# GateLoop attention and maxout FFN on one core: the first two groups' decay sums without TensorE's identity products, and every step list and PSUM room in another order

## The chip, the cores and the metric

One core of one Trainium2 chip runs the whole program in one launch. The metric is the device time of that launch in microseconds (us). Inputs and output are float32.

## The reference, cut to what matters

```python
# attention: batch 4, heads 8, seq 768, head_dim 48
mag = np.sqrt(a_re * a_re + a_im * a_im)
scale = np.minimum(mag, 0.999) / (mag + 1e-06)
a_re_n, a_im_n = a_re * scale, a_im * scale
for t in range(S):                                  # S_re, S_im: 48 x 48 per head
    S_re, S_im = ar * S_re - ai * S_im + kv, ar * S_im + ai * S_re   # kv = outer(k[t], v[t])
    y[:, :, t] = q[t] @ S_re
# feed-forward on x = y as (3072 tokens, 384); w1, w2, w3 are 384 x 768, w_out 768 x 384
h = np.maximum(np.maximum(x @ w1, x @ w2), x @ w3)
return h @ w_out
```

A complex gate of modulus below 1 decays and turns a state along the sequence. The kernel takes logarithms and angles of the gates, sums them along the tokens with matrix products, and turns the recurrence into products of scaled queries and keys inside chunks of 64 tokens, with a state carried from chunk to chunk.

## The kernel before, in words

**Tiling.** Work comes in 12 groups g (two pairs of batches, six pieces of 128 tokens each). A group has two columns, "x" and "y", one per batch. A tile is 128 tokens by 384 (one column) or 768 (both).

**Steps.** Every step is a word "name:group", and SCHEDULE is the list of all 1858 words. `program` (line 926) hands them to `run` (882) in order. Class `Bound` (98) ties each instruction to the one before it on its engine, so the list is the order on every engine: PE (TensorE), DVE (VectorE), ACT (ScalarE), POOL (GpSimd) and SP (the loads and stores). An engine that waits holds up all that stands behind it in its list.

The words of a group, in the order of the data:

- Lr, Li, Lq, Lk, Lv load (SP). Gates, in `gates` (413), halves 0 and 1 apart in group 0: sqr, sqi, add, lnL, expe, expw, lne, relu, Lnop (the decay's logarithm), and xor, abs, half, pw or addw, lnw, expL, mulai, mulw, stt, atan, turn (its angle). The angle needs modulus plus |a_re|: w + e in group 0, w + L in the others.
- Angles, in `angles` (496): cs sums them along the tokens on PE; t, nf, af reduce them to a turn; sa, sb are the sines (ACT). Cd carries a row to the next group.
- Decays, in `turns` (537): sums and F on PE; En, Ek, Eq, f0 to f3 exponentials on ACT; mk, mq, uk, uq, kEn scale keys and queries on DVE; tpk, tpq transpose on PE; Kc, Qc copy the result out of PSUM. Q1, Q2, KB, QB, QG, in `factors` (607), are DVE products.
- Scores, in `scores` (638): A and B on PE; g0 to g3 and b0, b1 put them under masks. State: dk on PE, h0 to h3 on DVE. y on PE, x the copy of it.
- Feed-forward: U11, U12, U01, U02 are x @ w on PE (`up`), u11 to u02 the copies and maxima into hT or xhx; each covers half of the 768 columns or, in group 0, a third for one column ("U22y:0": the last third, third matrix, column y; `up_one`, 761; the tile is hT). The output product of groups 1 to 11 is done by seven products P1 to P7 (with S1 to S4 and J before them, Px, Py for 128 of the inputs, and r1, r6, r75, r57, ox, oy after them) in `seven` (817). In group 0 it is Ox:0 and Oy:0, nine products of 384 columns each (`project`, 862): three on x itself with a product of weights that T and M made, then six on hT, two for each third. D stores.
- W words bring the four weight matrices in and round them (Wa, a cast by `weight_step`, 347; We; Wg an addition). Z words clear buffers.

**What sets the order.** Beside SCHEDULE there are three tables. SLOTS gives each PSUM tile one of four rooms, in the order in which `banks` (124) is called; a room is taken again only after its last reader. OTHER names words that run on the other engine of two: ACT or DVE for copies, casts, relu, abs; POOL or DVE for clears; and for additions:

```python
159     def increase(out, in_):
161         if other():
162             dve.tensor_tensor(out=out, in0=out, in1=in_, op=OP.add)
163         else:
164             pool.dma_start(out=out, in_=in_, accum_op=OP.add)
```

QUARTERS names words whose product is issued as four of 32 output columns instead of one of 128 (`mmf`, 117; also cs and F). It is empty before.

**The words of the change.** With SUMS = 2 (line 84), groups 0 and 1 form the sum of the modulus in PSUM: `pw` multiplies w and e (or L) by the identity matrix, and lnw and mulw read the sum there. The other groups add in place by addw.

Of the kernel before, what the change touches and what calls it, by code (L numbers as in the profile page):

```python
# [969 lines left out]
```

## Time and profile before

| | |
|---|---|
| median of 3 runs | 555.67 us (555.03 to 556.41) |
| profiled execution | 555.11 us |
| its span, first to last instruction | 553.4 us |
| mean granted clock of PE | 0.988 |
| busy: PE, DVE, ACT, POOL | 524.8, 470.8, 369.7, 70.7 us |
| instructions: PE, DVE, ACT, POOL | 10086, 728, 653, 117 |
| chain of waits that ended last | PE 84%, ACT 5%, SP's queue 5% |

How to read it: the span is 1.7 us shorter than the execution's own time, which includes what lies around it. Busy time is a mean over stages, and the stages differ: in the first 90 us loads, gates and weights are brought up, later all groups run as a pipeline. A float32 product shows as two matmul instructions in the trace, so that a word of four products counts 8. Each instruction has the line 107, where `Bound` issues it, so groups are told apart by tile names: output, then inputs, as in "op<-wo,hT". The number after an idle time, as in "[2.53 <-ACT L L107]", is how long the engine sat idle before the instruction, and whose result ended that.

### The profile page before, as it was taken

The page shows a single profiled execution, that of the slowest core. Times are in us where ns is not written, and L with a number is a line of the kernel's source. Part 1 is how long each engine was busy: PE and PEld are TensorE (multiplying, and loading weights), DVE is VectorE, ACT ScalarE, POOL GpSimd, SP SyncE. Part 2 cuts the span into 40 slices and gives each one's busy share as a digit, 9 for nine tenths or more (in the row PEclk, how much of TensorE's full clock was granted, in tenths as well). Part 3 has the DMA queues.
Part 4 walks back from the last instruction along what each step waited for, and adds up shares of the span by engine and source line. Part 5 has one row for each costly group of instructions (what it writes and reads, how often), then busy time and mean ns, then how long its engine had stood idle before and what let it go on. Part 6 is the DMA issues. An engine that isn't in the chain of part 4 may idle for free.

```text
span 553.4 us, 22672 instructions
## 1 busy us (share of the span) xinstructions
PE 524.8 (95%) x10086; PEld 449.1 (81%) x10086; DVE 470.8 (85%) x728; ACT 369.7 (67%) x653; POOL 70.7 (13%) x117
## 2 busy tenths in 40 slices
...
DVE  4788889999999997999988888999999998887432
...
GB/s 227 272 236 195 168 125 80 51 128 63 108 40 122 69 67 53 61 44 89 80 111 58 35 102 129 64 91 52 67 123 18 32 107 70 3 31 2 31 1 28
...
## 3 DMA queue, kind: packets, MB, share of 16 engines
...
q14 instruction: 18, 0.15, 0.1%
...
## 4 chain that ended last, share of the span: by engine, by line
PE 84%; ACT 5%; SPq 5%; DVE 2%; DMA 2%; issue 1%; DVEq 0%; ACTq 0%
PE up L107 33%; PE op L107 24%; PE y L107 7%; PE A L107 5%; SPq L107 5%; PE tp L107 4%; PE dk L107 3%; PE cs L107 3%; PE sums L107 2%; PE F L107 2%; PE B L107 1%; DMA ar<-in_a_re_dram 1%; ACT L L107 1%; ACT L107 1%; DMA ai<-in_a_im_dram 1%
## 5 line engine op out<-in xcount | busy, mean ns | idle before, releaser
L107 PE MATMUL up<-xhx,w 128*128 128x256 f32 x792 | 177.0, 382 | 0.1
L107 PEld LDWEIGHTS up<-xhx,w 128*128 128x128 f32 x792 | 148.9, 190 | 21.2 <-PE B L107 0.3
L107 ACT ACT_TABLE_LOAD x49 | 62.9, 1283 | 1.6 <-PEq L954 0.8
L107 ACT COPY atm<-B 32x128 f32<-32x128 f32 x96 | 24.5, 255 | 36.6 <-DVE atm L107 19.1
L107 PE MATMUL op<-wo,xhx 128*128 128x192 f32 (+1 forms) x220 | 48.6, 364 | 0.0
L107 DVE TENSOR_TENSOR Q<-Q,f 112x1024 f32<-112x1024 f32 (+1 forms) x48 | 45.4, 953 | 2.1 <-ACT Q L107 1.2
L107 POOL DMA_DIRECT2D ar<-nf x40 | 34.6, 1304 | 60.5 <-DVE ar L107 49.2
L107 ACT ACTIVATE f<-F 48x232 f32<-48x232 f32 x96 | 34.4, 359 | 10.3 <-PE F L107 6.3
L107 PEld LDWEIGHTS op<-wo,xhx 128*128 128x128 f32 x220 | 36.5, 190 | 4.8 <-issue 0.8
L107 PE MATMUL y<-atm,vb 128*32 128x64 f32 x1152 | 39.3, 222 | 0.1
L107 PE MATMUL y<-QG,g 112*32 112x64 f32 x1408 | 38.1, 219 | 0.3 <-issue 0.3
L107 PEld LDWEIGHTS y<-atm,vb 128*32 128x32 f32 x1152 | 32.5, 110 | 5.4 <-issue 2.9
L107 PEld LDWEIGHTS y<-QG,g 112*32 112x32 f32 x1408 | 34.9, 110 | 0.5 <-issue 0.5
L107 DVE TENSOR_TENSOR ot<-ot,op 128x384 f32<-128x384 f32 (+1 forms) x56 | 25.6, 465 | 10.7 <-PE op L107 6.4
L107 PE MATMUL op<-wo,strassen 128*128 128x192 f32 x176 | 33.0, 331 | 0.0
L107 POOL DMA_DIRECT2D Ln<-e x9 | 8.3, 923 | 192.0 <-ACT e L107 73.7
L107 DVE COPY_PREDICATED atm<-masko,A 128x256 f32<-128x256 uint8 x72 | 31.3, 436 | 1.7
L107 PE MATMUL op<-w,strassen 128*128 128x192 f32 x176 | 32.2, 329 | 0.0
L107 PE MATMUL A<-Q,K 112*32 112x80 f32 x1536 | 31.6, 234 | 0.2 <-DVE Q L107 0.2
L107 PEld LDWEIGHTS A<-Q,K 112*32 112x32 f32 x1536 | 27.3, 110 | 3.0 <-issue 1.6
L107 ACT COPY Q<-tp 112x1024 f32<-112x1024 f32 x22 | 22.3, 1015 | 10.7 <-PE tp L107 10.6
L107 PEld LDWEIGHTS op<-wo,strassen 128*128 128x128 f32 x176 | 28.8, 190 | 0.8
...
## 6 DMA issues: line engine op xcount, KB each, us to landing
...
Ln<-e POOLq DMA_DIRECT2D x9, 384.0 KB, 4.3
w<-L POOLq DMA_DIRECT2D x7, 384.0 KB, 4.5
```

The costliest lines, as they stand in the source:

```text
L107: ins = f(*a, **kw)
```

## The change

SUMS becomes 0. So pw0:0, pw1:0 and pw:1 leave, addw0:0, addw1:0 and addw:1 come, and lnw and mulw read w in SBUF. All four tables are new: SCHEDULE has 1858 words again, in another order; SLOTS has 301 entries for 304; OTHER 74 words for 45; QUARTERS 45 for none.

```diff
 SCHEDULE = """
...
+relu0:0 lne0:0 Lnop0:0 WL0:0 Wa0:0 lnL1:0 expe1:0 abs0:0 half0:0 addw0:0 expw1:0 xor1:0 lne1:0 relu1:0 Lnop1:0 lnw0:0
...
 OTHER = set("""
-Zf:0 Zg:0 afx:0 relu:1 Qcy:0 addw:2 Lnop:2 Wg8:0 u21y:0 addw:3 relu:4 afx:3 abs:4 Lnop:4 u01:2 xx:3 afy:4 afx:5 addw:6 u01:4 afx:6 afy:6 abs:7 relu:8 Kcy:6 afy:7 afx:7 relu:9 abs:9 u11:7 u01:7 afx:9 Kcx:9 xy:8 u11:8 Kcy:9 afy:10 abs:11 Kcx:10 Qcy:10 Kcy:11 Kcx:11 xy:11 u01:11 u11:11
+Zf:0 Z0:0 Z1:0 Wa0:0 addw0:0 addw1:0 Wa3:0 ty:0 Wa9:0 relu:1 Qcx:0 Zg:0 addw:1 afy:0 Qcy:0 addw:2 Wa7:0 Wg7:0 u21y:0
+Wa8:0 Wg8:0 afy:1 Lnop:2 ty:2 relu:3 abs:3 addw:3 Kcy:2 afx:3 r1:1 xy:2 tx:4 afx:4 afy:4 Qcx:4 r1:3 afy:5 addw:6 xx:4
+u11:4 tx:6 abs:7 r1:4 afx:6 xy:5 u11:5 addw:8 xx:6 xy:6 u11:6 afy:8 afx:8 xy:7 addw:9 r1:6 afy:9 relu:10 r1:7 u11:8
+r1:8 tx:10 afx:10 abs:11 addw:11 u01:9 r1:9 xy:10 ty:11 u11:10 afx:11 Qcx:11 u11:11 u01:11 r1:11
 """.split())
 
 QUARTERS = set("""
+csx:2 csy:3 csx:4 csy:4 csx:5 Py:3 Px:3 csx:6 P5:4 csy:6 Py:4 Px:4 csy:7 Px:5 Py:6 P4:6 Px:6 P3:6 U01:7 P1:7 P5:7 Px:7
+Py:7 P6:7 P4:7 csy:10 P5:8 P1:8 P7:8 P4:8 csx:10 U01:9 U02:9 P6:9 P2:9 csx:11 csy:11 U11:10 U01:10 Px:10 Py:10 P4:10
+P5:10 P6:10 P7:10
 """.split())
...
-    SUMS, ADDS = 2, 1
+    SUMS, ADDS = 0, 1
...
         elif name == "addw":
             if g >= SUMS:
-                increase(w, L)
+                increase(w, L if g >= ADDS else e)
```

What the tables do is seen in the instructions, in program order on an engine. DVE near its start, group 0's gates, before (w<-pw,L is mulw; w_124 is a weight's We; ai and ar are the gates' parts):

```order
L107 ISA L<-L,e 128x384
L107 SCALAR_TENSOR_TENSOR ai<-ar,ai 128x384
L107 TENSOR_SCALAR ar<-ar 128x384
L107 SCALAR_TENSOR_TENSOR w_124<-w_125,xhx 128x3x256
L107 SCALAR_TENSOR_TENSOR Ln_111<-L,e 128x384
L107 SCALAR_TENSOR_TENSOR ai<-ar,ai 128x384
L107 SCALAR_TENSOR_TENSOR w_124<-w_126,xhx 128x3x256
L107 TENSOR_TENSOR w<-pw,L 128x384
```

and now, from the first Lnop to the second mulw:

```order
L210 SCALAR_TENSOR_TENSOR Ln_111<-L,e 128x384
L210 TENSOR_SCALAR xhx<-w_125 128x768
L210 TENSOR_SCALAR ar<-ar 128x384
L210 TENSOR_TENSOR w<-w,e 128x384
L210 SCALAR_TENSOR_TENSOR ai<-ar,ai 128x384
L210 SCALAR_TENSOR_TENSOR Ln_111<-L,e 128x384
L210 SCALAR_TENSOR_TENSOR w_124<-w_125,xhx 128x3x256
L210 TENSOR_TENSOR w<-w,e 128x384
L210 TENSOR_TENSOR w<-w,L 128x384
L210 TENSOR_TENSOR ai<-ai,L 128x384
```

The two sums w<-w,e are DVE additions, and a cast of the weights (xhx<-w_125, word Wa0) stands on DVE where ACT had it.

PE around Oy:0, before (the rows ahead of these are dkx:1; then tpqy:1, Ax:1, Oy:0, Fx:2, Bx:1, Ay:1):

```order
L107 MATMUL tp<-ident,uq_97 112x64 x16
L107 MATMUL A<-Q_121,K_119 32x80 x32
L107 MATMUL op<-wo,ot 128x384 x3
L107 MATMUL op<-wo,hT 128x384 x6
L107 MATMUL F<-cuts,Ln_111 48x29 x16
L107 MATMUL B<-QB,KB 32x32 x16
```

and now (Fy:1, U02y and U12y, U11y, tpkx:1, tpqx:1, U22y, Oy:0, tpqy:1, tpky:1, Ax:1, csx:2 in quarters, U22x, U21x):

```order
L210 MATMUL up<-ot,w_126 128x128 x12
L210 MATMUL up<-ot,w_125 128x128 x6
L210 MATMUL tp<-ident,uk_95 112x64 x16
L210 MATMUL tp<-ident,uq_96 112x64 x16
L210 MATMUL up<-ot,w_126 128x128 x6
L210 MATMUL op<-wo,ot 128x384 x3
L210 MATMUL op<-wo,hT 128x384 x6
L210 MATMUL tp<-ident,uq_97 112x64 x16
L210 MATMUL tp<-ident,uk_93 112x64 x16
L210 MATMUL A<-Q_121,K_119 32x80 x32
L210 MATMUL cs<-w,upto 32x192 x8
L210 MATMUL up<-ot,w_126 128x128 x6
```

Two transposes, Ax:1, a cs and two up words that stood ahead of Oy:0 now stand behind it, as do, out of these rows, dkx:1, sumsx:2, csy:2 and U12x.

PE's end, group 11, before (U01 and U11, U02, then P1, Px, P2, P5, P6, Py, P3, P7, P4):

```order
L107 MATMUL up<-xhx,w_125 128x256 x18
L107 MATMUL up<-xhx,w_126 128x256 x9
L107 MATMUL op<-wo,xhx 128x192 x4
L107 MATMUL op<-wo,xhx 128x384
L107 MATMUL op<-wo,xhx 128x192 x4
L107 MATMUL op<-wo,strassen 128x192 x4
L107 MATMUL op<-w_124,strassen 128x192 x4
L107 MATMUL op<-wo,xhx 128x384
L107 MATMUL op<-wo,strassen 128x192 x4
L107 MATMUL op<-w_124,strassen 128x192 x4
L107 MATMUL op<-w_124,xhx 128x192 x4
```

and now (U11, U12, Px, U01, U02, P7, P2, P5, P6, P1, Py, P3, P4):

```order
L210 MATMUL up<-xhx,w_126 128x256 x9
L210 MATMUL op<-wo,xhx 128x384
L210 MATMUL up<-xhx,w_125 128x256 x9
L210 MATMUL up<-xhx,w_126 128x256 x9
L210 MATMUL op<-w_124,strassen 128x192 x4
L210 MATMUL op<-wo,xhx 128x192 x4
L210 MATMUL op<-wo,strassen 128x192 x4
L210 MATMUL op<-w_124,strassen 128x192 x4
L210 MATMUL op<-wo,xhx 128x192 x4
L210 MATMUL op<-wo,xhx 128x384
L210 MATMUL op<-wo,strassen 128x192 x4
L210 MATMUL op<-w_124,xhx 128x192 x4
```

Px stands between the up words, and P7 is the first of the seven; P4 stays the last.

More of the change, by code (lines that the diff above doesn't have):

```diff
@@ new lines @@
+mkx:0 relu:1 sumsy:0 Eny:0 uqx:0 Wa6:0 We6:0 expe:1 expw:1 f2x:0 WL1:0 ukx:0 tpqx:0 tpkx:0 Qcx:0 f3x:0 abs:1 lne:1
+Zg:0 Lnop:1 Kcx:0 kEnx:0 Lvx:0 WL10:0 half:1 Eqy:0 addw:1 Lky:0 WL11:0 Lrx:2 Lry:2 afy:0 Eky:0 mqy:0 Q1x:0 Q2x:0 T0:0
+t0:0 lnw:1 expL:1 mulw:1 mulai:1 Cdx:0 dkx:0 Cdy:0 T1:0 Wa10:0 t1:0 M0:0 T2:0 QBx:0 We10:0 M1:0 stt:1 Wa11:0 Liy:2
+say:0 We11:0 mky:0 t2:0 h1x:0 h2x:0 Wa1:0 h3x:0 We1:0 QGx:0 sby:0 uqy:0 sqr:2 atan:1 WL2:0 Lix:2 Wa2:0 sqi:2 Fy:0
+f3y:0 add:2 lnL:2 f1y:0 Ax:0 M2:0 g0x:0 We2:0 Wg2:0 f2y:0 WL4:0 Wa4:0 f0y:0 m0:0 uky:0 tpky:0 tpqy:0 Kcy:0 g1x:0
@@ new lines @@
+turn:1 g2x:0 g3x:0 KBx:0 Bx:0 Qcy:0 WL5:0 Lvy:0 m1:0 b1x:0 relu:2 kEny:0 b0x:0 xor:2 Z3:0 Wg1:0 We4:0 Q1y:0 Wg4:0
+Q2y:0 csy:1 ty:1 csx:1 expw:2 Wa5:0 We5:0 Wg5:0 tx:1 yx:0 expe:2 xx:0 Lqy:1 WL7:0 Lky:1 sumsx:1 lne:2 QBy:0 nfx:1
+nfy:1 WL8:0 Lqx:1 Ay:0 g0y:0 abs:2 Eqx:1 afx:1 sumsy:1 half:2 dky:0 KBy:0 g1y:0 Enx:1 Eny:1 Ekx:1 Eqy:1 QGy:0 addw:2
+g2y:0 g3y:0 h1y:0 Eky:1 h2y:0 h3y:0 Cdy:1 Z4:0 Lkx:1 lnw:2 expL:2 mulai:2 Liy:3 Lix:3 mulw:2 stt:2 Lix:4 U02x:0 U01x:0
+u01x:0 By:0 b1y:0 U11x:0 b0y:0 yy:0 atan:2 Wa7:0 Cdx:1 We7:0 Wg7:0 sbx:1 Fx:1 xy:0 turn:2 u02x:0 mky:1 mqx:1 sax:1
@@ new lines @@
+u11x:0 sby:1 f2x:1 mkx:1 uqx:1 Lqx:2 Z2:0 Lvx:1 Lvy:1 Liy:4 U01y:0 f0x:1 u01y:0 f1x:1 U21y:0 u21y:0 Fy:1 ukx:1 mqy:1
+f1y:1 f0y:1 f3y:1 U02y:0 U12y:0 Wa8:0 We8:0 f2y:1 Wg8:0 f3x:1 u02y:0 h0x:1 h0y:1 afy:1 U11y:0 u11y:0 u12y:0 Lnop:2
+tpkx:1 tpqx:1 Qcx:1 QBx:1 Q1x:1 Q2x:1 U22y:0 QGx:1 u22y:0 Oy:0 Kcx:1 sqi:3 say:1 uqy:1 tpqy:1 uky:1 tpky:1 kEny:1 oy:0
+Qcy:1 Kcy:1 Q2y:1 Ax:1 g0x:1 Q1y:1 csx:2 tx:2 nfx:2 afx:2 U22x:0 U21x:0 g1x:1 g2x:1 g3x:1 u21x:0 sbx:2 KBx:1 u22x:0
+kEnx:1 Ay:1 Bx:1 b1x:1 b0x:1 dky:1 h1y:1 g0y:1 U12x:0 u12x:0 h2y:1 h3y:1 dkx:1 sumsx:2 Lry:3 Lkx:2 Lky:2 QBy:1 Lrx:3
@@ new lines @@
+sqi:4 Fy:2 atan:3 turn:3 add:4 b1x:2 f0y:2 f3y:2 lnL:4 h1x:2 h2x:2 mqy:2 b0x:2 f1y:2 f2y:2 h3x:2 Lrx:5 uqy:2 Lqy:3
+Lry:5 Dx:0 U12:1 u12:1 tpky:2 tpqy:2 csx:3 Qcy:2 Kcy:2 QBy:2 Q2y:2 tx:3 nfx:3 yx:2 xx:2 csy:3 expe:4 P1:1 S1:1 P5:1
+Q1y:2 KBy:2 kEny:2 lne:4 ty:3 nfy:3 Ay:2 By:2 S2:1 g0y:2 relu:4 afx:3 expw:4 Px:1 P6:1 P2:1 Py:1 afy:3 abs:4 g1y:2
+S4:1 g2y:2 g3y:2 sby:3 h0y:2 b1y:2 sax:3 b0y:2 xor:4 half:4 sbx:3 Lvy:2 dky:2 J4:0 sumsx:3 S3:1 P4:1 P7:1 P3:1 h1y:2
+h2y:2 QGy:2 h3y:2 Ekx:3 mkx:3 Eqx:3 r1:1 Lnop:4 Lvy:3 Dy:0 r6:1 r75:1 yy:2 ox:1 r57:1 Enx:3 oy:1 addw:4 lnw:4 say:3
@@ new lines @@
+expL:4 Cdx:3 Cdy:3 Fy:3 Fx:3 f2y:3 f1x:3 sumsy:3 f3y:3 Eqy:3 f3x:3 xy:2 U01:2 Eky:3 Eny:3 mulai:4 mqx:3 ukx:3 f2x:3
+f0y:3 sqr:5 mqy:3 uqy:3 mulw:4 Lky:3 stt:4 sqi:5 add:5 mky:3 uky:3 u01:2 uqx:3 U02:2 u02:2 f1y:3 h0y:3 f0x:3 tpky:3
+tpqx:3 tpqy:3 tpkx:3 Kcy:3 kEnx:3 S3:2 Qcx:3 Dx:1 Q1x:3 Qcy:3 Q1y:3 atan:4 Q2x:3 Q2y:3 QGx:3 QBx:3 turn:4 Lry:6 Kcx:3
+U11:2 lnL:5 u11:2 U12:2 u12:2 KBx:3 csx:4 csy:4 tx:4 expe:5 ty:4 nfy:4 expw:5 Ax:3 Bx:3 g0x:3 nfx:4 g1x:3 sby:4 relu:5
+afx:4 abs:5 sbx:4 sax:4 addw:5 P1:2 P7:2 S1:2 g2x:3 KBy:3 Lky:4 P5:2 Lqx:4 Dy:1 g3x:3 S2:2 Lqy:4 dkx:3 h0x:3 h1x:3
@@ new lines @@
+h0x:4 sqr:6 add:6 U01:3 u01:3 KBx:4 kEny:4 QGx:4 lnL:6 U02:3 csy:5 Lqy:5 Lky:5 Lvx:4 QBx:4 dkx:4 u02:3 S1:3 ty:5 nfy:5
+Fy:4 f3y:4 f1y:4 S2:3 f0y:4 f2y:4 h1x:4 h2x:4 Ax:4 csx:5 tx:5 Lqx:5 expe:6 Q2y:4 g0x:4 g1x:4 h3x:4 nfx:5 Q1y:4 afx:5
+relu:6 lne:6 Lnop:6 P7:3 P6:3 P5:3 S4:3 P1:3 Bx:4 g2x:4 g3x:4 KBy:4 QBy:4 xor:6 Ay:4 Py:3 Px:3 Dx:2 expw:6 abs:6 r1:3
+b0x:4 afy:5 b1x:4 addw:6 g0y:4 g1y:4 say:5 r6:3 r75:3 sax:5 lnw:6 yx:4 xx:4 Lix:7 g2y:4 half:6 Lvy:4 Lkx:5 r57:3 h0y:4
+g3y:4 QGy:4 P4:3 P3:3 P2:3 By:4 b1y:4 dky:4 sumsx:5 oy:3 h1y:4 b0y:4 expL:6 yy:4 ox:3 Ekx:5 Eqx:5 sumsy:5 mulai:6
@@ new lines @@
+mqx:5 xy:4 mulw:6 Eky:5 mky:5 sqi:7 mkx:5 stt:6 Lvy:5 Enx:5 h2y:4 h3y:4 atan:6 sby:5 U01:4 sbx:5 ukx:5 uqx:5 sqr:7
+Eqy:5 Lvy:6 turn:6 Lry:8 uky:5 xor:7 U02:4 Fx:5 add:7 u01:4 f1x:5 f3x:5 f0x:5 f2x:5 h0x:5 mqy:5 u02:4 uqy:5 Lrx:8
+Lky:6 Lvx:5 U11:4 u11:4 Dy:3 Eny:5 tpqx:5 Qcx:5 tpky:5 S3:4 tpkx:5 tpqy:5 Kcx:5 Q2x:5 Qcy:5 Kcy:5 Q1x:5 QBx:5 QGx:5
+kEnx:5 U12:4 u12:4 S1:4 KBx:5 Fy:5 dkx:5 f1y:5 f0y:5 S2:4 h1x:5 Ax:5 csx:6 tx:6 f2y:5 nfx:6 g0x:5 g1x:5 f3y:5 g2x:5
+Q2y:5 g3x:5 h0y:5 Liy:8 P5:4 Q1y:5 Lix:8 lnL:7 csy:6 ty:6 expw:7 Bx:5 P1:4 P6:4 relu:7 P7:4 expe:7 abs:7 KBy:5 b1x:5
@@ new lines @@
+Kcx:6 QBx:6 Kcy:6 Q2x:6 Qcy:6 Lrx:9 kEny:6 csx:7 Q1y:6 sqr:8 tx:7 nfx:7 sbx:7 KBx:6 U02:5 P1:5 u02:5 S1:5 S2:5 Ax:6
+add:8 g0x:6 csy:7 ty:7 Bx:6 lnL:8 expe:8 P6:5 P7:5 kEnx:6 P5:5 g1x:6 g2x:6 KBy:6 g3x:6 lne:8 expw:8 b0x:6 b1x:6 Dy:4
+nfy:7 Q2y:6 dkx:6 afy:7 QGx:6 S4:5 Ay:6 Px:5 Dx:4 r1:5 r6:5 g0y:6 r75:5 g1y:6 afx:7 g2y:6 relu:8 g3y:6 P3:5 Py:5 P2:5
+r57:5 QBy:6 By:6 h1x:6 h2x:6 yx:6 abs:8 addw:8 xx:6 say:7 sby:7 QGy:6 b1y:6 h3x:6 P4:5 oy:5 b0y:6 lnw:8 half:8 Cdy:7
+Cdx:7 dky:6 h1y:6 h2y:6 sumsy:7 Eky:7 Lix:9 Lqx:7 Lky:7 ox:5 Eqy:7 Eny:7 yy:6 xy:6 Fx:7 f1x:7 sumsx:7 Ekx:7 h3y:6
@@ new lines @@
+mky:7 uky:7 mkx:7 U01:6 expL:8 mulw:8 mulai:8 f0x:7 Enx:7 Eqx:7 f2x:7 mqx:7 mqy:7 stt:8 sax:7 uqx:7 ukx:7 Lvx:7 uqy:7
+atan:8 U11:6 u01:6 f3x:7 u11:6 h0x:7 Liy:9 Lix:10 Dy:5 tpkx:7 tpqx:7 tpky:7 Kcx:7 Lvy:8 tpqy:7 Qcx:7 Lkx:8 turn:8
+Lry:10 KBx:7 kEnx:7 Q2x:7 sqi:9 U12:6 Q1x:7 Lnop:8 sqr:9 Qcy:7 add:9 u12:6 Fy:7 dkx:7 Kcy:7 f3y:7 QBx:7 f1y:7 kEny:7
+h1x:7 h2x:7 h3x:7 f2y:7 f0y:7 Q2y:7 sumsx:8 Eqx:8 Enx:8 Ekx:8 U02:6 Q1y:7 u02:6 lnL:9 Ax:7 g0x:7 relu:9 g1x:7 g2x:7
+g3x:7 QGx:7 Bx:7 KBy:7 b0x:7 b1x:7 Py:6 P4:6 QBy:7 csx:8 csy:8 tx:8 nfx:8 Ay:7 Px:6 g0y:7 ty:8 nfy:8 afy:8 S1:6 yx:7
@@ new lines @@
+xx:7 g1y:7 g2y:7 S3:6 By:7 Lqy:8 P2:6 expe:9 h0y:7 Lqx:8 afx:8 lne:9 sax:8 g3y:7 S2:6 xor:9 Lvy:7 P7:6 P5:6 P6:6 Dx:5
+S4:6 QGy:7 dky:7 say:8 b0y:7 b1y:7 h1y:7 Liy:10 mqx:8 sbx:8 uqx:8 h2y:7 P3:6 h3y:7 sby:8 yy:7 Lky:8 xy:7 mkx:8 ukx:8
+expw:9 abs:9 half:9 Cdy:8 addw:9 lnw:9 expL:9 Lrx:10 Lqx:9 Lvy:9 P1:6 r1:6 r6:6 r75:6 r57:6 U11:7 u11:7 ox:6 Fx:8
+f0x:8 oy:6 mulw:9 f2x:8 f1x:8 tpqx:8 tpkx:8 mulai:9 Qcx:8 kEnx:8 f3x:8 QBx:8 h0x:8 sqi:10 Kcx:8 U01:7 Q2x:8 stt:9
+QGx:8 u01:7 Lvx:8 sumsy:8 dkx:8 Eny:8 Fy:8 Eqy:8 mqy:8 h1x:8 h2x:8 h3x:8 Cdx:8 Lnop:9 Eky:8 f2y:8 KBx:8 uqy:8 mky:8
@@ new lines @@
+Q1x:8 atan:9 sqr:10 add:10 f3y:8 f1y:8 lnL:10 uky:8 U12:7 u12:7 U02:7 f0y:8 turn:9 tpqy:8 tpky:8 Qcy:8 u02:7 S1:7
+Kcy:8 S3:7 Q2y:8 csy:9 csx:9 tx:9 Ax:8 Q1y:8 ty:9 nfy:9 sby:9 g0x:8 P7:7 g1x:8 nfx:9 g2x:8 Ay:8 Bx:8 QBy:8 S2:7 g3x:8
+b1x:8 afy:9 say:9 b0x:8 expe:10 KBy:8 g0y:8 g1y:8 P1:7 relu:10 P5:7 S4:7 afx:9 g2y:8 g3y:8 kEny:8 Px:7 Py:7 yx:8 P6:7
+expw:10 abs:10 addw:10 Dx:6 r1:7 Dy:6 By:8 b0y:8 xx:8 b1y:8 sbx:9 P2:7 P3:7 dky:8 sumsx:9 Ekx:9 Enx:9 Eqx:9 r6:7 r75:7
+r57:7 lne:10 QGy:8 Lky:9 Lry:11 h0y:8 xor:10 half:10 Cdx:9 h1y:8 P4:7 oy:7 h2y:8 yy:8 ox:7 xy:8 h3y:8 lnw:10 expL:10
```

51 lines of the change are left out of this document (46 added, 5 removed).

## The prediction

> **What bounds the kernel now.** I read the head of the page first, then its slices, then the busy time of each engine in chosen stretches (columns: stretch, its length, busy us of PE, PE's weight loads, DVE, ACT and POOL, granted clock, DMA share, GB/s).
>
> ```profile
> span 553.4 us, 22672 instructions
> PE 524.8 (95%) x10086; PEld 449.1 (81%) x10086; DVE 470.8 (85%) x728; ACT 369.7 (67%) x653; POOL 70.7 (13%) x117
> ...
> DVE  4788889999999997999988888999999998887432
> ```
> ```profile
> 0.00:10.00 10.00, 0.85 (x33) 0.83 (x33) 2.99 (x10) 7.11 (x15) 7.71 (x34) 1.00 0.84 224
> 10.00:20.00 10.00, 7.96 (x46) 4.03 (x46) 6.05 (x11) 9.60 (x22) 7.94 (x20) 0.83 0.95 251
> 20.00:30.00 10.00, 4.32 (x48) 3.27 (x47) 9.07 (x16) 9.97 (x14) 0.00 (x0) 0.97 0.92 244
> ...
> 92.00:152.00 60.00, 59.52 (x1252) 48.68 (x1244) 58.43 (x92) 46.55 (x85) 5.09 (x6) 1.00 0.46 87
> 152.00:238.00 86.00, 85.82 (x1787) 74.48 (x1785) 78.32 (x124) 66.60 (x112) 9.16 (x11) 1.00 0.34 67
> 238.00:538.00 300.00, 299.78 (x5810) 264.37 (x5807) 257.10 (x393) 172.18 (x312) 24.99 (x30) 1.00 0.31 62
> 538.00:553.40 15.40, 10.58 (x60) 9.42 (x58) 5.32 (x10) 0.32 (x1) 0.00 (x0) 1.00 0.08 26
> ```
> ```profile
> 0.00:93.19 93.19, 70.29 (x1198) 52.87 (x1199) 72.77 (x116) 85.27 (x147) 31.49 (x70) 0.93 0.81 189
> ```
>
> The reader is to see two stages. From 92 to 538 us PE is busy 445.1 of 446 us: nothing shortens that stage but less PE work or an earlier start. Up to 93.19 us PE has 22.9 us of idle time, ACT is full from 10 us on, and DVE idles 20.4 us, 10.96 of them in the first 20. So the end is the time at which PE's gapless stretch can begin, plus the PE work left there, plus the tail.
>
> As the mark between the stages I take the first group's output product, Oy:0: nine products, the last two of which need the rectified sum that DVE writes as u22y:0.
>
> ```profile
> 85.29 0.87 PE L107 MATMUL cs<-w,upto 128*64 128x192 f32 x8
> 86.09 3.10 PE L107 MATMUL up<-ot,w 128*128 128x128 f32 x24
> 89.12 1.14 PE L107 MATMUL dk<-vb,uk 64*64 64x48 f32 x64
> 90.19 0.66 PE L107 MATMUL tp<-ident,uq 64*112 64x64 f32 x16
> 90.79 1.31 PE L107 MATMUL A<-Q,K 112*32 112x80 f32 x64
> 92.03 2.20 PE L107 MATMUL op<-wo,ot 128*128 128x384 f32 x6
> ```
> ```profile
> 94.07 4.04 PE L107 MATMUL op<-wo,hT 128*128 128x384 f32 x12
> ```
> ```profile
> 92.79 0.40 DVE L107 TENSOR_TENSOR hT<-hT,up 128x256 f32<-128x256 f32 x1
> ```
>
> The six products on hT take 4.04 us, 0.66 each (start to start), so the last two begin at 94.07 + 4 x 0.66 = 96.7. DVE is done at 93.19: 3.5 us to spare.
>
> **The change, part by part.**
>
> **1. The identity products.** pw0:0, pw1:0 and pw:1 go.
>
> ```profile
> L107 PE MATMUL pw<-w,ident x8: 486/844/1007, 9.9 to 37.1; 128*128 128x384 f32 x8
> ```
> ```profile
> 15.48 1.48 PE L107 MATMUL pw<-w,ident 128*128 128x384 f32 x2 [2.04 <-ACT f L107]
> ```
>
> They lie between 9.9 and 38 us; 16 instructions of 0.486 to 1.007 us duration, in a stage where PE waits anyway. Their time is not on the path: I count 0 us (bounds: 0 to 10 us off PE, and the second only if PE bound that stage, which its 22.9 idle us deny). In their place DVE adds two 384-column tiles and one of 768 columns. They are not transfers: all three words stand in OTHER.
>
> **2. PE work behind the mark.** Nine words that PE did ahead of Oy:0 now come behind it: U12x, U21x, csx:2, csy:2, sumsx:2, tpky:1, tpqy:1, dkx:1, Ax:1. By the starts in the rows above, two up words are 3.03 us, a cs word 0.80, dk 1.07, tp 0.60, A 1.24; sums is 0.68 by this piece of the chain of waits:
>
> ```profile
> 198.82 0.68 PE sums L107 x16
> ```
>
> Sum 3.03 + 1.60 + 0.68 + 1.20 + 1.07 + 1.24 = **8.8 us more behind the mark**. Against it stand fewer changes of array shape: from Oy:0 on, consecutive words of unlike shape fall from 158 to 137, partly by order and partly because 45 words are issued in 32-column quarters.
>
> ```profile
> 155.78 1.50 PE op L107 x8
> ...
> 181.16 5.42 PE op L107 x32
> ```
>
> Four 192-column words take 5.42, one 1.50: three more cost 3.92, 1.31 each, so a change after such a run is 0.19 us. The mixed words behind the mark have no row that separates theirs so cleanly; I take a little less. 21 x 0.15 = **3.1 us less** (bounds 1, if a drained array hides behind loads, to 4.2 at 0.20). Left over: +5.7 us. [...]
>
> The quarters' own stream time I take as unchanged. Before has no quartered op; the nearest row is the y product, four 32-column tiles side by side:
>
> ```profile
> 152.40 1.72 PE y L107 x112
> ```
>
> 112 instructions with 112 loads of 32 columns in 1.72 us is 15 ns for each, though one load lasts 110 ns:
>
> ```profile
> L107 PEld LDWEIGHTS y<-atm,vb 128*32 128x32 f32 x1152 | 32.5, 110 | 5.4 <-issue 2.9
> ```
>
> So loads need not hold it up; a quartered op issues 32 in 1.31 us. Bounds: 0, to the rival below.
>
> **3. The tail.**
>
> ```profile
> 537.91 9.12 PE op L107 x52
> ...
> 547.05 0.57 DVE ot L107
> ...
> 547.64 0.56 DVE ot L107
> ...
> 548.25 1.58 PE op L107 x8
> ```
>
> PE waits 1.2 us for a PSUM room that two DVE sums free, before its last product. Now Px runs between the up words and P7 and P6 stand early, so rooms are freed further ahead; the last product keeps its place and the sum and the store behind it are the same. **-1.2 us** (bounds -1.2 to +0.6, one such DVE step waiting in a new place).
>
> Together: the end moves by (last two products of Oy:0 now) - 96.7 + 5.7 - 1.2. It breaks even if they start at 92.2.
>
> **4. When the mark is reached.** DVE's list ahead of u22y:0 grows. Prices, start to start, are about 0.08 below these mean durations:
>
> ```profile
> L107 DVE TENSOR_TENSOR QG<-Q,f 112x1024 f32<-112x1024 f32 (+1 forms) x24 | 27.1, 1130 | 0.0
> L107 DVE TENSOR_TENSOR w<-w,L 128x768 f32<-128x768 f32 x13 | 12.4, 953 | 0.3 <-ACT L L107 0.2
> ...
> L107 DVE COPY Q<-tp 112x1024 f32<-112x1024 f32 x2 | 2.4, 1222 | 0.5 <-PE tp L107 0.5
> ...
> L107 DVE TENSOR_SCALAR Ln<-L 128x768 f32<-128x768 f32 x4 | 2.2, 553 | 0.0
> ...
> L107 DVE MEMSET vb<- 128x768 f32 x2 | 1.4, 698 | 0.2
> ```
>
> New there: three adds 0.47 + 0.47 + 0.87; five weight casts (Wa) at 0.47 by the TENSOR_SCALAR row; two clears 0.62 each; Qcx 1.14; QGx:1 1.14; Wg7 0.87; h0y:1 0.47 and four small angle steps 0.27: 10.0 with rounding. Gone to behind the mark: three 768-column products, two nf, one mask, small ones, 5.2. Net **+4.8**, to 76.5 us from 71.8 (by starts). The casts are not shown on DVE before; a 768-column step there lies between 0.55 and 0.95 us, so +0 to +2 more.
>
> ACT's list ahead of the mark shrinks from 82.7 us of work by starts (its 85.27 busy us above, less overlaps) to 66.1: the five casts, two Q copies, two K copies and the angle and exponential steps of groups 1 and 2 stand on DVE or behind the mark now. A cast is
>
> ```profile
> 8.31 1.07 ACT L107 ACTIVATE xhx<-w 128x768 f16<-128x768 bf16 x1
> ```
>
> and DVE's idle time was mostly waiting on ACT:
>
> ```profile
> 5.50 0.56 DVE L107 CUSTOM_DVE_ANT_0 L<-L,e 128x384 f32<-128x384 f32 x1 [2.53 <-ACT L L107]
> 8.44 0.56 DVE L107 SCALAR_TENSOR_TENSOR Ln<-L,e 128x384 f32<-128x384 f32 x1 [2.38 <-ACT L L107]
> ...
> 17.70 0.56 DVE L107 TENSOR_TENSOR w<-pw,L 128x384 f32<-128x384 f32 x1 [2.34 <-ACT L L107]
> ```
>
> I take 9 us of idle for 20.4: the clears fill the start, and gate steps no longer queue behind casts on ACT, such as the one at 8.31. Bounds: 5 (no gate can reach DVE before 5.5) to 20.4 as now. DVE then does u22y:0 at 76.5 + 9 = 85.5, and PE starts the two products some 0.5 later, at 86.0. End: 86.0 - 96.7 + 5.7 - 1.2 = **-6.2 us**.
>
> **5. Given back.** From 92 to 152 DVE is busy 58.43 of 60 us, 1.6 to spare. A start 6 us earlier with a DVE list longer by some 10 us over the whole run makes PE wait there somewhere; what is queued behind such a wait is all of PE's list. I take **+2 us** (bounds 0 to 6).
>
> Sum: -4.2 against the profiled execution, whose own time is 555.11 us beside its span of 553.4; it would be 550.9. The median of before is 555.67, 0.56 above it, so 551.4.
>
> **The rivals.**
>
> (a) DVE keeps up everywhere, or idles only 5 us: without the +2, 549.5; with idle 5 another 4 less, 545.5. For it: ACT's 16.6 us fewer. Against: the slices of DVE stand at 9 from the seventh to the fifteenth, 83 to 207 us.
>
> (b) DVE becomes the bound. Place: DVE's list up to u22y:0. Price: its idle stays at 20.4, so the mark is 76.5 + 20.4 = 96.9, the products 97.4, and the end 97.4 - 92.2 = +5.2 us: 560.9. It decides from the mark later than 91.7, that is, idle over 15.2; each us more is a us of the kernel. For it: the loads of q, k and a run at a DMA share of 0.84 to 0.95 in the first 30 us, so gates can wait for data however free ACT is. Against: the rows above name ACT.
>
> (c) Idle around 12 and DVE late by 4 us in the busy stretch: all given back, -6.2 + 3 + 4 = +0.8, 556.5, and with a us either way 554 to 557.3.
>
> (d) The change doesn't do what it says: the sums as accumulating transfers, not adds. In before such a transfer lands 4.5 us after its issue, on the path of the first gates:
>
> ```profile
> w<-L POOLq DMA_DIRECT2D x7, 384.0 KB, 4.5
> ```
>
> Three of them are 13.5 us, less the DVE adds' 1.8; with a third of it on the path the mark comes 4 us later, and -4.2 + 4 leaves 555.5. The order shows adds, so this has little.
>
> (e) Quartered loads are not hidden: 32 loads of 0.110 us would make a 192-column word 3.5 us, +2.2 for each of 17, and the up words' 72 loads +3.8 for each of 5; with the rest some 58 us, 609. The y row, 15 ns a load in the same shape, speaks against it. [...]
>
> **How the numbers follow.** A measurement of this kernel can tell about 0.3%, 1.7 us: faster is below 554.0, slower above 557.3. Chances: forecast 0.52, (a) 0.13, (b) 0.17, (c) 0.15, (d) 0.02, (e) 0.01. Faster is forecast + (a), 0.65; within, (c) + (d), 0.17; slower, (b) + (e), 0.18. The range leaves out the far ends of (a) and (b): 546.5 to 558.5. Predicted: 551.4.
>
> **What would show it.** u22y:0 on DVE at 84 to 88 us with DVE idle under 12 before it (step 4); PE without gaps from there, DVE-caused waits of about 2 us between 90 and 200 (5); no gap ahead of PE's last product (3); one op word in quarters 1.3 us long and PE busy about 520 in all (2). The forecast is wrong if the mark comes later than 91 us, or if PE shows waits over 4 us behind it.

## The result, and the profile after

The changed kernel takes 551.87 us (median of 4 runs, 550.04 to 552.60) beside 555.53 for the kernel before on the same chip: a ratio of 0.9927, 95% interval 0.9899 to 0.9956. Measured once more, beside other executions of the kernel before, it took 551.40 for 554.40, a ratio of 0.9954 (0.9928 to 0.9980). So it is faster by 0.5 to 0.7%; 551.4 was forecast.

The head of the page and its slices, after:

```profile
span 550.9 us, 24305 instructions
PE 516.8 (94%) x10910; PEld 440.7 (80%) x10910; DVE 482.4 (88%) x757; ACT 367.9 (67%) x636; POOL 68.8 (12%) x112
...
DVE  6999798989999989989978999999979899989533
```

PE's busy time fell by 8.0 us, DVE's rose by 11.6, and the span fell by 2.5. DVE now stands at 6 tenths in the first slice and at 9 in the next three, where it stood at 4, 7, 8 and 8.

Busy time up to the mark (the end of u22y:0), the columns as before:

```profile
0.00:10.00 10.00, 0.61 (x8) 0.60 (x12) 5.60 (x15) 7.55 (x18) 7.69 (x32) 1.00 0.81 192
10.00:20.00 10.00, 3.10 (x52) 2.12 (x46) 9.89 (x19) 8.81 (x18) 8.77 (x20) 1.00 1.01 240
...
0.00:87.84 87.84, 59.84 (x974) 47.10 (x975) 77.39 (x124) 72.82 (x129) 30.82 (x67) 0.96 0.84 197
```

DVE is idle for 10.45 us ahead of the mark (20.4 before); in the first 20 us it idles 4.5 (10.96 before). The mark itself on DVE, and Oy:0 on PE:

```profile
87.42 0.42 DVE L210 TENSOR_TENSOR hT<-hT,up 128x256 f32<-128x256 f32 x1
```
```profile
84.23 2.10 PE L210 MATMUL op<-wo,ot 128*128 128x384 f32 x6
86.16 4.03 PE L210 MATMUL op<-wo,hT 128*128 128x384 f32 x12
```

Oy:0 starts 7.8 us earlier than before. Its last two products start at 86.16 + 4 x 0.66 = 88.8 (96.7 before). DVE was done with the mark at 87.84, 1.0 us ahead of them (3.5 before), so PE did not wait for it. The end of the chain of waits:

```profile
529.94 6.91 PE up L210 x32
536.85 9.77 PE op L210 x58
546.62 0.02 issue
546.64 0.55 DVE ot L210
547.20 0.27 DVEq L1068
547.46 0.26 DVE ot L210
```

There is no gap ahead of the last product any more, and PE ends at 546.62 (549.83 before): 3.2 us earlier.

What PE waited for, from 55 us on (columns: what waited, for whom; us in total, times, longest):

```profile
PE dk L210 <- issue: 3.6, 1, 3.6
PE A L210 <- ACT ot L210: 1.5, 1, 1.5
PE y L210 <- issue: 1.3, 2, 0.8
PE up L210 <- ACT ot L210: 1.0, 1, 1.0
PE sums L210 <- issue: 0.2, 1, 0.2
PE op L210 <- DVE nf L210: 0.2, 1, 0.2
```

Two things in this list matter. PE stood still for 5.1 us, most of it in the middle of words, with "issue" as the cause: it waited for nothing that the profile shows. Before, the same list has 0.8 us of that. And DVE, which was forecast to hold PE back for 2 us, did so for 0.2.

### The profile page after: what moved, and what is told of

Read it like the earlier page. It is cut to its first block, busy times and chain, and to the rows that moved or that the text cites. A ratio compares the mean times of both kernels' runs of the same rounds, so it can differ in the third digit from the quotient of the medians.

```text
span 550.9 us, 24305 instructions
## 1 busy us (share of the span) xinstructions
PE 516.8 (94%) x10910; PEld 440.7 (80%) x10910; DVE 482.4 (88%) x757; ACT 367.9 (67%) x636; POOL 68.8 (12%) x112
## 3 DMA queue, kind: packets, MB, share of 16 engines
q8 instruction: 86, 1.41, 1.0%
## 4 chain that ended last, share of the span: by engine, by line
PE 85%; ACT 4%; SPq 4%; DMA 3%; issue 2%; DVE 1%; DVEq 0%; ACTq 0%
PE up L210 34%; PE op L210 24%; PE y L210 7%; PE A L210 5%; PE dk L210 4%; SPq L210 4%; PE tp L210 4%; PE sums L210 3%; PE cs L210 2%; PE F L210 2%; PE B L210 1%; DMA wo<-in_moe_w_dram 1%; DMA strassen<-in_moe_w_out_dram 1%; DMA ai<-in_a_im_dram 1%; ACT L210 1%
## 5 line engine op out<-in xcount | busy, mean ns | idle before, releaser
L210 PE MATMUL up<-xhx,w 128*128 128x256 f32 (+1 forms) x1062 | 178.0, 382 | 0.0
L210 PEld LDWEIGHTS up<-xhx,w 128*128 128x128 f32 (+1 forms) x1062 | 144.8, 163 | 25.8 <-issue 1.0
L210 PE MATMUL op<-wo,xhx 128*128 128x192 f32 (+3 forms) x358 | 50.1, 380 | 0.2 <-DVE nf L210 0.2
L210 DVE TENSOR_TENSOR Q<-Q,f 112x512 f32<-112x512 f32 (+1 forms) x48 | 44.9, 953 | 0.8 <-ACT Q L210 0.7
L210 PEld LDWEIGHTS op<-wo,xhx 128*128 128x128 f32 (+1 forms) x358 | 35.0, 149 | 3.8 <-issue 0.9
L210 PE MATMUL op<-wo,strassen 128*32 128x192 f32 (+1 forms) x296 | 32.8, 328 | 0.0
L210 PE MATMUL op<-w,strassen 128*32 128x192 f32 (+1 forms) x296 | 32.1, 328 | 0.0
L210 PEld LDWEIGHTS dk<-vb,uk 64*48 64x48 f32 (+1 forms) x1408 | 24.6, 133 | 7.5 <-issue 6.9
L210 PE MATMUL dk<-vb,uk 64*64 64x48 f32 (+1 forms) x1408 | 27.1, 223 | 3.6 <-issue 3.6
L210 DVE TENSOR_TENSOR QG<-Q,f 112x1024 f32<-112x1024 f32 (+1 forms) x24 | 27.2, 1132 | 3.5 <-PE y L210 3.5
```

The costliest lines, as they stand in the source:

```text
L210: ins = f(*a, **kw)
```

## The experiments

Each kernel is the changed one with one edit, or the kernel before where that is said. The first four ask which part of the change carries the time, and whether the 3.6 us stall belongs to the kernel.

**again**: no edit.

> The changed kernel once more, nothing altered. In its first profile PE stood still for 3.6 us at 59.42 us in the middle of a dk word, with no semaphore to wait for, and ran at a granted clock of 0.56 to 0.67 for some 6 us behind it. If that stall belongs to the kernel, this profile shows it in the same place and the time is 551 to 553 us. If it comes and goes from one execution to the next, this profile may lack it; then u22y:0 comes 2 to 3 us earlier than 87.4 and the profiled execution takes 549 to 550 us.

551.40 us. The stall is there again, at 59.39 us and for 4.1 us, ahead of the same instruction of dky:0. It belongs to the kernel. PE's waits inside y at 110 and 114 us, 1.3 us in all, are not in this profile, so those come and go.

**no_quarters**

```diff
 QUARTERS = set("""
-csx:2 csy:3 csx:4 csy:4 csx:5 Py:3 Px:3 csx:6 P5:4 csy:6 Py:4 Px:4 csy:7 Px:5 Py:6 P4:6 Px:6 P3:6 U01:7 P1:7 P5:7 Px:7
...
 """.split())
```

> QUARTERS emptied, all else as in the changed kernel. My theory: a change of array shape costs PE 0.15 to 0.19 us and nothing hides it where PE has no gaps. Without quarters the changes from Oy:0 on go from 137 to 179, 42 more, so 6.3 to 8 us longer: 558 to 560 us. Rival one: the quarters do nothing (loads or drains hide): 552 us. Rival two: quartered loads cost time, then the kernel gets faster without them: below 550 us.

570.99 us, a ratio of 1.0284 (1.0244 to 1.0323) to before: 19.6 us slower than the changed kernel, over twice what any theory gave.

```profile
PE 523.8 (93%) x10070; PEld 446.2 (79%) x10070; DVE 483.9 (85%) x757; ACT 367.5 (65%) x636; POOL 68.7 (12%) x112
```
```profile
95.00:535.00 440.00, 430.49 (x8827) 370.31 (x8820) 389.11 (x608) 291.38 (x502) 37.99 (x45) 1.00 0.33 63
```
```profile
PE y L208 <- issue: 4.5, 7, 1.8
PE sums L208 <- issue: 2.7, 3, 1.0
PE dk L208 <- DMA vb<-in_v_dram: 1.6, 1, 1.6
PE dk L208 <- issue: 0.4, 1, 0.4
PE B L208 <- issue: 0.3, 1, 0.3
```

PE is busy 8.4 us more than in the profile of "again" (515.4). From Oy:0 on it is 9.3 us (469.28 for 459.99) for 42 more changes of shape, at most 0.22 us each. Part of it may belong to the idle gaps that follow here: the kernel "shifted_by_144" below has the same changes as "again", 13.2 us of such gaps, and is busy 4.3 us more (464.30). In proportion, 7.9 us of gaps would make 2.6 us of the 9.3 and leave 0.16 for a change, an estimate. Another 9.5 us is idle time between 95 and 535 us: 7.9 of it are "issue" waits in the middle of words, 1.6 a late load of v. The rival of unhidden loads is refuted by the changed kernel itself, in whose chain three quartered words of 192 columns stand together:

```profile
425.44 3.90 PE op L210 x96
```

They take 1.30 us each, as a whole word does (1.31): the 32 loads of 32 columns in each, 0.110 us long by the profile, are hidden. Without the quarters PE also has 1680 records fewer (20140 for 21820), which matters for the theory below, so this run alone does not say what the quarters are worth.

**sums_as_transfers**

```diff
 OTHER
-addw0:0 addw1:0 addw:1
```

> The three new sums leave the list of words that run on DVE, so they become accumulating transfers on POOL's queue. My theory: the gates of groups 0 and 1 wait for a landing of 4 to 6 us each where a DVE addition takes 0.5 or 0.9; with a third to a half on the path, u22y:0 comes 2 to 5 us later and the kernel takes 554 to 557 us. Rival: the path to u22y:0 does not go through these sums, and DVE is 1.8 us shorter: 550 to 552 us.

572.50 us, 1.0311 (1.0277 to 1.0345). What ACT and POOL did at the first sum:

```profile
11.12 0.51 ACT L211 ACTIVATE L<-L 128x384 f32<-128x384 f32 x1
23.90 0.52 ACT L211 ACTIVATE L<-w 128x384 f32<-128x384 f32 x1 [12.27 <-DMA w<-e]
```
```profile
16.27 1.03 POOL L211 DMA_DIRECT2D w<-e  x1
25.93 0.86 POOL L211 DMA_DIRECT2D w<-e  x1 [8.62 <-ACT e L211]
```

The sum was ready to be formed at 10.92 us, where DVE adds it in the changed kernel. As a transfer it is issued at 16.27, behind POOL's preparation of constants, and ACT, whose next step is the logarithm of it, stands still for 12.27 us with all that is queued behind. The second transfer waits for a step of that queue. My price, a landing of some 5 us with part of it on the path, had left out both queues. Oy:0 starts at 103.22, 18 us later than in "again" (85.05).

**two_weight_adds_on_dve**

```diff
 OTHER
+Wg4:0 Wg5:0
```

> Wg4 and Wg5, two additions of weight blocks which POOL issues as accumulating transfers at 54.73 and 57.33 us, run on DVE instead. If PE's stall at 59.42 us is an instruction fetch held up by the transfers (DMA share 1.19 at 54 to 60 us), it shrinks to under 1 us: 3 us saved, 1.7 us of DVE work added, so 550 to 551 us. If the transfers have nothing to do with it, the stall stays and the kernel takes 552 to 554 us.

551.25 us, 0.9937 (0.9910 to 0.9965): no different from the changed kernel. The stall in dky:0 shrank from 4.1 to 1.6 us, not to under 1. In the profile Oy:0 starts 3.6 us earlier than in "again" (81.44 for 85.05), but PE's last product ends only 0.8 us earlier: PE waits 2.1 us by "issue" between 95 and 535 us (0.3 in "again"). In the changed kernel the instruction queue's packet came 1.2 us after PE had stopped, with the DMA engines at this load (third and last but one columns: PE busy, DMA share):

```profile
54.00:60.00 6.00, 3.90 (x155) 3.15 (x144) 6.00 (x10) 6.00 (x12) 2.54 (x3) 1.00 1.19 192
60.00:63.01 3.01, 0.00 (x0) 0.00 (x0) 2.83 (x6) 0.72 (x2) 3.01 (x6) 0.78 1.11 294
63.01:69.00 5.99, 5.99 (x68) 5.90 (x69) 2.98 (x5) 2.44 (x4) 1.16 (x2) 0.54 1.08 243
```

Here, with two transfers fewer, the packet came at 59.99, 0.6 us earlier than in the changed kernel (60.62), and before PE stopped at 61.17. But PE itself stopped 1.8 us later, since it had waited for DVE, which now had the two additions to do:

```profile
PE sums L211 <- DVE nf L211: 1.5, 1, 1.5
```

So most of the shorter stall is PE's later arrival. That the load on the DMA engines makes the fetch late is not shown: in "shifted_by_32" below, at a share of 1.21 between 54 and 60 us, the packet came at 57.16 and this stall is absent. With the shorter stall, the low clock behind it is absent too: two up words take 2.94 us here at a granted clock of 1.00. In the changed kernel they take 4.87 right behind the stall, at 0.54, and 2.95 later:

```profile
64.46 4.87 PE L210 MATMUL up<-ot,w 128*128 128x128 f32 x24
```

**A theory for the stalls.** The instruction queue moved 86 packets and 1.41 MB after, 79 and 1.29 MB before:

```profile
q8 instruction: 86, 1.41, 1.0%
```

That is 16 KB a packet, and PE's 10910 products with as many loads come to 254 records for each (before: 20172 / 79 = 255). I counted PE's records ahead of each gap in the middle of a word. In "no_quarters" the counts, for "issue" gaps of 0.3 us and more from 60 us on, are 1202, 6033, 6540, 8323, 9595, 10103, 11628, 14425, 15693, 16712, 17474; modulo 256 they run 178, 145, 140, 131, 123, 119, 108, 89, 77, 72, 66, a slow drift along one lattice: from 1202 to 17474 is 64 steps of 254.25 records. In the changed kernel the gaps at 110 and 114 us lie at 2980 and 3236, 256 apart. With all of PE's records counted, those of semaphores too, they lie at 3009 and 3265, the stall in dky:0 at 1217, and the gap of before at 100.83 us at 2753: each is 193 modulo 256. So the theory is that PE fetches its instructions in pieces of 256 and stands still where a piece runs out before the next has come. By the starts of the packets, the next fetch begins 1.1 us (before) and 1.4 us (after) behind a piece's first record, in the median, and what it brings can be used some 2 us later, an estimate (the gaps listed here end 2.2 to 2.8 us after a packet's start, one 3.3); a piece filled with y, A, dk and F lasts less than that (224 records of y take 1.72 us), one with up and op words far longer (72 records of up words take 8.04 us at 413.30).

If so, the same order of work costs more or less time by where the borders fall. The next experiments move the borders by quartering early words, and test the parts of the change with the borders held as nearly as that allows.

**shifted_by_144, shifted_by_32, shifted_by_248**

```diff
 QUARTERS                        # one line each, in this order
+M0:0 M1:0
+csx:0 csy:0
+M0:0 M1:0 M2:0 csx:0 csy:0
```

> The changed kernel with M0:0 and M1:0 issued in quarters too: the same PE stream time, at 34 to 42 us, where PE waits for others, but 144 more PE instructions ahead of all the rest. My theory, formed on the runs before: PE fetches its instructions in pieces of 16 KB, 256 instructions, and stands still where a piece has run out in under some 3 us (dense words such as y, A, dk) before the next has come; what the order does to the time depends on where the piece borders fall. By the times of the pieces in the traces, a shift by 144 puts many more borders behind dense words: 5 to 9 us of PE stalls in the middle of words, 556 to 561 us. Rival: the stalls in the middle of words are DMA contention or chance; then the time stays at 550 to 552 us.

> The changed kernel with csx:0 and csy:0 in quarters: 32 more PE instructions ahead of the rest. Fetch theory: the borders move part of the way towards dense words; by the times of the pieces the stalls grow to between a third and a half of what 144 gave: 556 to 562 us. Rival: within 1.5 us of the changed kernel.

> The changed kernel with M0, M1, M2, csx:0 and csy:0 in quarters: 248 more PE instructions ahead of all the rest, eight short of a whole piece of 256. It quarters the two words of the run shifted by 144 and three more. Fetch theory: the borders fall 8 instructions from where the changed kernel has them, so the 19 us that the shift by 144 cost are gone: 550 to 553.5 us, at most 2.5 us of PE gaps in the middle of words from 70 us on. Rival: the quartered M words themselves, or the number of instructions, cost the time; then 568 us or more.

They took 570.32 (1.0289, 1.0260 to 1.0317), 556.78 (1.0044, 1.0018 to 1.0070) and 552.75 us (0.9948, 0.9916 to 0.9981). PE in the stretch from 95 to 535 us, for each in that order:

```profile
95.00:535.00 440.00, 426.06 (x9662) 366.76 (x9662) 389.71 (x610) 291.74 (x503) 37.99 (x45) 1.00 0.33 64
```
```profile
95.00:535.00 440.00, 433.91 (x9558) 371.93 (x9557) 389.77 (x609) 290.42 (x496) 38.06 (x45) 1.00 0.33 64
```
```profile
95.00:535.00 440.00, 438.89 (x9752) 377.92 (x9749) 395.73 (x620) 292.94 (x504) 38.06 (x45) 1.00 0.33 65
```

13.9, 6.1 and 1.1 us of idle time (0.55 in "again"). A shift by nearly a whole piece, with more quartered words than the shift by 144, has nearly the old time (552.75 for 551.40): the border's place decides, not the words. The counts ahead of the gaps lie on the old lattice (3236, 6289, 9851, 17481 in the shift by 144: 164, 145, 123, 73 modulo 256) while the work has moved along it. The shift by 144 costs 19 us in the medians, where I had said 5 to 9, and 16.5 in the profiled executions. There the idle time in this stretch is 13.4 us more, nearly all of it such gaps, and PE is counted busy 4.2 us more.

The shift by 32 shows something else as well. The border falls 32 records earlier in dky:0, the packet for it comes at 57.16 us (60.62 in the changed kernel), and the stall is absent: dky:0 starts at 59.43 (58.92 in the changed kernel), and yet Oy:0 starts 5.1 us earlier than in "again" (85.05):

```profile
79.99 2.10 PE L210 MATMUL op<-wo,ot 128*128 128x384 f32 x6
```

So the changed kernel itself loses some 5 us ahead of Oy:0 to this one stall, and the shift by 32 gains them there and loses more behind. Why the packet comes so late in the changed kernel stays open.

**before_with_adds, before_with_adds_same_borders**: the kernel before with the sums as DVE additions in the places of pw; in the second, the 32 PE instructions (16 matmuls and their 16 loads) that go with pw are made up. The three PSUM rooms of pw leave SLOTS in both.

```diff
-    SUMS, ADDS = 2, 1
+    SUMS, ADDS = 0, 1
...
-pw0:0 pw1:0 pw:1
+addw0:0 addw1:0 addw:1          # in SCHEDULE and in OTHER
...
 QUARTERS                        # the second kernel alone
+csx:0 csy:0
```

> The kernel before with one part of the change alone: SUMS 0, the three sums as DVE additions in the places of pw, its own order otherwise. First prediction's view: pw is not on the path and DVE has 1.8 us more, so 0 to +1 us against before. Rival one: PE bounds the kernel, so 5 us less PE work is 3 to 5 us less time. Rival two, the fetch theory: without pw, 32 PE instructions are gone ahead of all the rest, and the borders of the 16 KB pieces move by 32 towards dense words: some 4 us more PE stalls in the middle of words, so 3 to 5 us slower than before.

> As the run with the additions in the kernel before, but csx:0 and csy:0 in quarters, which adds 32 PE instructions near the start, so that the borders of the 16 KB pieces lie where they lay in before. Fetch theory and first prediction agree: 0 to +1 us against before, and no more than 1 us of PE gaps in the middle of words from 70 us on. Rival (PE work bounds): 3 to 5 us faster than before, here and in the run without quarters alike.

564.02 us (1.0166, 1.0140 to 1.0193) and 557.80 (1.0055, 1.0036 to 1.0075). PE from 95 to 535 us in the first and the second:

```profile
95.00:535.00 440.00, 432.04 (x8770) 375.44 (x8769) 388.92 (x599) 284.10 (x506) 39.23 (x47) 1.00 0.34 67
```
```profile
95.00:535.00 440.00, 439.49 (x8846) 382.41 (x8835) 391.59 (x604) 285.85 (x508) 39.23 (x47) 1.00 0.35 67
```

8.0 and 0.5 us idle. Of the 9.5 us that the additions cost in the old order, 6.2 are borders by these two times. The other 3.3 are the first stage: Oy:0 starts at 95.58 for 92.03. In the first kernel it starts at 93.51, so this division holds to some 2 us only, and quartering csx:0 and csy:0 may have a part in the 3.3. Both of my theories had 0 to +1 there, so both are off by 2 us; the rival by which 5 us less PE work is 3 to 5 us less time is refuted. The old order with this part of the change alone is slower than before.

**after_with_products, products_in_group_0_alone**: the other way round, pw back in the new order, for both groups or for group 0.

```diff
-    SUMS, ADDS = 0, 1
+    SUMS, ADDS = 2, 1           # group 0 alone: 1, 1
...
-addw0:0 addw1:0 addw:1
+pw0:0 pw1:0 pw:1                # group 0 alone: the first two
...
 SLOTS                           # rooms 6, 4, 4 for them
 QUARTERS
+M0:0 M1:0 M2:0
```

> The changed kernel with the identity products back in place of the three additions (PSUM rooms 6, 4, 4), and M0, M1, M2 in quarters, so that 248 more PE instructions stand ahead: nearly a whole piece of 256, the borders almost where they were. My view: PE has the room for 5 us more before 55 us, DVE has 1.8 us less, lnw waits for PE instead; the time is within 2 us of the changed kernel, 549.5 to 553.5. Rival: the gain of the change is the 5 us of PE work that it removes; then 555 us or more.

> The changed kernel with the identity products back in group 0 alone (SUMS 1, PSUM rooms 6 and 4), group 1's sum a DVE addition as in the changed kernel; M0, M1, M2 in quarters, so that 232 more PE instructions stand ahead, 24 short of a piece, where the times of the pieces give no more stalls than now. With all three products back the kernel took 561 us, and DVE stood still for 6.2 us at 35.4 waiting for group 1's logarithm behind pw:1. If that one product is the cost, this run takes 551 to 554 us. [...]

561.08 us (1.0110, 1.0077 to 1.0144) and 558.38 (1.0054, 1.0025 to 1.0084). The first shows a wait that I had not priced. The last of the three products on PE, and DVE behind it:

```profile
33.52 1.65 PE L229 MATMUL pw<-w,ident 128*128 128x384 f32 x2 [2.45 <-ACT Ek L229]
...
37.52 0.99 PE L229 MATMUL pw<-L,ident 128*128 128x384 f32 x2
```
```profile
41.63 0.96 DVE L229 TENSOR_TENSOR w<-pw,L 128x768 f32<-128x768 f32 x1 [6.21 <-ACT L L229]
```

Group 1's product stands behind a wait for Ek in PE's list and takes 5 us for four products at a granted clock of 0.67 (30 to 42 us); DVE waits 6.21 us for the logarithm after it, and Oy:0 starts at 91.74. With group 0's products alone it starts at 83.15, so these cost the first stage nothing. That kernel is slow for another reason: 7.1 us of PE idle time between 95 and 535 us. I had taken a shift of -24 instructions for harmless by the times of the pieces; it is not. My count of the pieces' times says where stalls grow, and not to a few us how much.

**casts_on_act**

```diff
 OTHER
-Wa0:0 Wa3:0 Wa9:0 Wa7:0 Wa8:0
```

> The changed kernel with the five weight casts Wa0, Wa3, Wa9, Wa7, Wa8 on ACT again; PE's instructions are untouched. My theory of the first stage: gate steps queue behind such casts on ACT (1.0 us each) and DVE waits for them, so u22y:0 comes 2 to 4 us later though DVE has 2.4 us less: 553 to 556 us. Rival: DVE itself bounds that stage, and gets 2.4 us less: 549 to 551 us.

556.76 us (1.0031, 1.0006 to 1.0056): 5.4 us more than the changed kernel, and a little more than the 553 to 556 that my theory gave. DVE's waits up to the mark:

```profile
DVE w L211 <- ACT xhx L211: 4.8, 2, 3.8
DVE g L211 <- ACT g L211: 3.7, 2, 3.1
DVE L L211 <- ACT L L211: 3.4, 3, 1.5
DVE ar L211 <- ACT e L211: 2.7, 1, 2.7
DVE w L211 <- ACT w L211: 1.7, 1, 1.7
DVE wo L211 <- ACT xhx L211: 1.5, 1, 1.5
```

DVE waits for the casts themselves (xhx, 6.3 us in all) and for gate steps behind them; u22y:0 comes at 95.03, 7.6 us later than 87.42 where I had said 2 to 4, with less work on DVE (the execution profiled, 558.91, is the slowest of the ten). With these five casts back on ACT, the change is no gain over the kernel before.

None of the versions beats the changed kernel: "two_weight_adds_on_dve" and "shifted_by_248" are level with it, and the others are slower.

## Why the prediction was right, point by point

The time, 551.4, was right within 0.5 us, and the path was right: PE reaches Oy:0 earlier because DVE waits less for ACT, and pays part of that back as work behind it. Step 3 held, step 4 came 2.8 us short, steps 2 and 5 together took 1.9 us less than forecast, 5 by another mechanism; and one hazard, the piece borders, was not in it at all. That the sum came so close is in part luck, since these errors nearly cancel.

**Step 1** (pw off the path, 0 us). Right for group 0, by "products_in_group_0_alone". Not right for group 1 in the new order, where the product costs 8.6 us at Oy:0 (91.74 less 83.15). In the old order, additions in its place cost 3.3 us. So the removal is worth nothing by itself; with the order around it, it is part of the earlier mark.

**Step 2** (+5.7 us behind the mark). From the start of Oy:0 to PE's last product before took 549.83 - 92.03 = 457.8 us, now 546.62 - 84.23 = 462.4: +4.6, where steps 2, 3 and 5 give +6.5. PE's busy time in it rose by 4.9 us (455.67 to 460.59), where step 2 has 5.7. So of the 8.8 us of words moved behind the mark 3.9 came back, not 3.1. One count was off: 158 changes are those from dkx:1 on; from Oy:0 on before has 155, 18 more than now. The price of a change was low: 3.9 us for 18 is 0.22 each, at the top of what "no_quarters" allows, for the 0.15 taken. The two errors work against each other. No run shows an array that drains, by which step 2 has its lower bound of 1 us; what the runs show is this price of a change, 0.16 to 0.22 us. That the quarters cost no stream time is shown by the three words in 3.90 us.

**Step 3** (-1.2). Right: the gap is gone.

**Step 4** (the mark at 85.5, the two products at 86.0). They came at 87.8 and 88.8. DVE's work up to there was 77.4 us and its idle time 10.45 (9 forecast). The 76.5 us of work in the forecast does not compare with that: it adds to 71.8 us, counted from start to start, idle time counted by the profile's busy time, and 71.8 + 20.4 is 92.2, not the 93.19 at which the mark ended before. On one measure the work is 72.8 + 4.8 = 77.6 us, and the forecast mark would have been 86.6. The work was therefore right; about 1 us of the miss is this sum, and about 1.5 is idle time. That the idle time halves because casts leave ACT is shown by "casts_on_act". The 1.5 us of idle time I put down to the stall in dky:0: DVE waits 2.2 us for g at 65.10, ACT's copy of what dk makes. With the stall at 1.6 us, in "two_weight_adds_on_dve", Oy:0 starts at 81.44, 3.6 us earlier than in "again", though DVE has two additions more; without it, in "shifted_by_32", at 79.99. The mark alone did not set the time of the two products, as the working has it: PE's last wait ahead of them is 1.0 us for ACT's ot, at 74.03, and from there its own list took it to 88.8.

**Step 5** (+2, DVE late between 90 and 200 us). The mechanism was wrong, and the size, within its bounds, was half of that. PE idles 1.79 us between 95 and 535 us (0.88 before), so 0.9 us is given back, 1.3 of the 1.79 at piece borders in y. Only 0.2 belongs to DVE, which kept up.

Sum: Oy:0 starts 7.8 us earlier, +4.6 as step 2 has it: PE ends 3.2 us earlier; the last sums and the store, which step 3 took as unchanged, took 0.7 us more, so the span fell by 2.5 in this execution, where 4.2 was forecast. The median fell by 3.7, since the execution profiled (552.60) is the slowest of the four.

**The rivals.** (a) came true in its mechanism, DVE keeping up, but not in its time, since the mark was late. (b) and (c) did not come. (d), transfers for additions, was priced at 555.5 and takes 572.5. (e) is refuted.

What stays open: why 12 executions of the changed kernel spread over 7.2 us (548.14 to 555.35 in "again") where 18 of the kernel before, run beside them, spread over 3.6; 31 more, run later, spread over 6.2. The fetches, some of which come late in one profile and not in the next, would do that; it was not tried. What the quarters are worth with the borders held was not tried either.
